# Joining 64-bit weights to fp32 with one join moved from VectorE to ScalarE

## The chip, the cores and the metric

One core of one Trainium2 chip runs the whole program. The metric is device time in microseconds of one execution. The kernel before took 991.16 us, the median of three runs (989.19 to 991.88).

## The reference

A linear-attention block and two MLPs on 2304 tokens of 512 features (batch 4, 8 heads, sequences of 576, head size 64, 128 random features):

```python
kv = np.einsum('bhsm,bhsd->bhmd', k_p, v)            # k_p, q_p = phi(k), phi(q): exp of a projection
out = np.einsum('bhsm,bhmd->bhsd', q_p, kv) / (np.einsum('bhsm,bhm->bhs', q_p, z)[..., None] + 1e-06)
x = ((x @ w_a) * (x @ w_b)) @ w_out                  # first MLP, d_ff 1536
h = np.maximum(x @ w_in, 0.0); y = (h * h) @ w_out2  # second MLP, d_ff 2048
```

The weights of both MLPs are the product of an fp32 array and an fp64 scalar, and so arrive as fp64. All products are wanted at fp32 quality.

## The kernel before

TensorE multiplies in fp32r, a rounded fp32. So each weight is cut in two parts, hi (its value cast to fp32r) and lo (the rest), and each product is made of three matmuls (hi·hi, hi·lo, lo·hi). Activations are cut in the same way.

**From fp64 to fp32.** A weight lies in memory as two 32-bit words. The kernel loads both (the tile raw, last index 0 for the low word, 1 for the upper) and puts the fp32 together from bits. ScalarE reads the upper word as if it were an fp32, scales it by a power of two (WORD_SCALE), and so shifts the exponent into place; the result is the tile a. VectorE then makes the tile p in three joins: a shifted left by 3 with the lowest bits masked off (`tensor_scalar`, line 187), the sign of a joined to it (line 191), and the three top bits of the low word (line 195, shifted right by 29). Then ScalarE casts p to hi (line 199) and VectorE subtracts to get lo (line 200).

**First MLP.** `split` does this, for 1024 elements a partition (the pair of w_a and w_b of one f) or 512 (one f of w_out). 12 f make 12 big and 12 small splits. `load_split` issues the loads on the sync engine SP into one of two raw buffers and puts the split on a list; the splits are spread over the first 175 us, beside the attention of the first batches and the first passes of the MLP. The tiles a and p have one buffer each. The order in which instructions stand on each engine is set by a list scheduler when the program is built. The work that stands beside the splits is: transposes of q and k that ScalarE copies out of PSUM (S, line 382), their projection (ps_p, line 329), minimum on VectorE (nm, line 333), exponential on ScalarE (qp and kp, line 335), transposes of qp copied out (qT, line 543), products with kv (ps_n, line 548) and quotients on VectorE; and of the MLP ab (line 696), the product a·b on ScalarE and VectorE (lines 800 to 803) and y (line 721). The kept hi and lo of w_a and w_b stay in the tile W; those of w_out go to a scratch in DRAM.

**Second MLP.** It uses a seven-product form of the matrix product. `unit` converts one j of w_in or w_out2 in two halves of 512 elements (lines 919 to 930, the same three joins into the area AB), makes four differences (line 939), and casts and subtracts each of seven blocks (lines 950 and 953). There are 16 units, so 32 halves. Eight units are made in the last pass of the first MLP (540 to 640 us) and eight in `in_step` (640 to 800 us), where ScalarE also copies the products pY and pW out of PSUM (line 1035) and VectorE adds (line 1038). From 800 us on the last product runs (line 1184), without units.

Of the kernel before, what the change touches and what calls it, by code (L numbers as in the profile page):

```python
# [11 lines left out]
U32 = mybir.dt.uint32  # L12
ACTF = mybir.ActivationFunctionType
ALU = mybir.AluOpType
# [10 lines left out]


WORD_SCALE = 2.0 ** -111
W_SCALE = 2.0 ** 8
Y_SCALE = 2.0 ** -24

# [5 lines left out]
def f32(ap):  # L36
    return ap.bitcast(F32)


def i32(ap):  # L40
    return ap.bitcast(I32)


@with_exitstack
def kernel(
# [13 lines left out]
    nc = tc.nc  # L59
# [119 lines left out]
    def split(raw, t):  # L179

        n = raw.shape[1]
        a = top["cut"].tile([128, 2, 512], F32, tag="a", name="a")[:, 0:n]
        p = top["cut"].tile([128, 2, 512], F32, tag="p", name="p")[:, 0:n]
        nc.scalar.activation(out=a, in_=f32(raw[:, :, :, 1]), func=ACTF.Copy, scale=WORD_SCALE)
        nc.vector.tensor_scalar(
            out=i32(p), in0=i32(a), scalar1=3, scalar2=0x7FFFFFF8,
            op0=ALU.logical_shift_left, op1=ALU.bitwise_and,
        )  # L190
        nc.vector.scalar_tensor_tensor(
            out=i32(p), in0=i32(a), scalar=-0x80000000, in1=i32(p),
            op0=ALU.bitwise_and, op1=ALU.bitwise_or,
        )
        nc.vector.scalar_tensor_tensor(
            out=p.bitcast(U32), in0=raw[:, :, :, 0].bitcast(U32), scalar=29,
            in1=p.bitcast(U32), op0=ALU.logical_shift_right, op1=ALU.bitwise_or,
        )
        nc.scalar.copy(out=t[:, :, 0, :], in_=p)  # L199
        nc.vector.tensor_tensor(  # L200
            out=t[:, :, 1, :], in0=p, in1=f32(t[:, :, 0, :]), op=ALU.subtract
        )
# [482 lines left out]
    def a_units():  # L685
# [80 lines left out]
        for n, (pi, f) in enumerate(todo):  # L766
# [27 lines left out]
            for o in range(0, g.shape[2], w_):  # L794
# [3 lines left out]
                else:  # L798
                    a_s = gpool.tile([128, w_], F32, tag="t", name="a_s", bufs=2)
                nc.scalar.mul(out=a_s, in_=aps[:, c], mul=1.0 / W_SCALE)  # L800
                nc.vector.tensor_tensor(out=a_s, in0=bps[:, c], in1=a_s, op=ALU.mult)  # L801
# [84 lines left out]
    def raw_at():  # L886
        return area["raw"][:, 0:2048].rearrange("p (h f w) -> p h f w", h=2, w=2)
# [17 lines left out]
    def unit(kind, j, dst, groups, nxt=None, stage=None):  # L905


        raw = raw_at()
        a = seg("AB", 0, 2, 512)
        bt = seg("AB", 4096, 8, 256)  # L910

        def load(h):
            unit_load(*nxt, h)

        ops = []
        for h in range(2):
            w = bt[:, 2 * h:2 * h + 2].rearrange("p a n -> p (a n)")
            ops += [
                lambda h=h: nc.scalar.activation(
                    out=f32(a[:, h]), in_=f32(raw[:, h, :, 1]), func=ACTF.Copy, scale=WORD_SCALE,  # L920
                ),
                lambda h=h, w=w: nc.vector.tensor_scalar(
                    out=i32(w), in0=i32(a[:, h]), scalar1=3, scalar2=0x7FFFFFF8,
                    op0=ALU.logical_shift_left, op1=ALU.bitwise_and,
                ),
                lambda h=h, w=w: nc.vector.scalar_tensor_tensor(
                    out=i32(w), in0=i32(a[:, h]), scalar=-0x80000000, in1=i32(w),
                    op0=ALU.bitwise_and, op1=ALU.bitwise_or,
                ),
                lambda h=h, w=w: nc.vector.scalar_tensor_tensor(  # L930
                    out=w.bitcast(U32), in0=raw[:, h, :, 0].bitcast(U32), scalar=29,
                    in1=w.bitcast(U32), op0=ALU.logical_shift_right, op1=ALU.bitwise_or,
                ),
            ]
            if nxt:
                ops.append(lambda h=h: load(h))

        def sub(o, x, y):
            nc.vector.tensor_tensor(
                out=f32(bt[:, o]), in0=f32(bt[:, x]), in1=f32(bt[:, y]), op=ALU.subtract  # L940
            )

        ops += [lambda t=t: sub(*t) for t in ((4, 0, 2), (6, 1, 0), (5, 1, 4), (7, 3, 5))]
        fill = []
        for g0, g1 in groups:
            o = {}

            def hi(g0=g0, g1=g1, o=o):
                o["t"] = dst(g0, g1)
                nc.scalar.copy(out=o["t"][:, :, 0], in_=f32(bt[:, 1 + g0:1 + g1]))  # L950

            def lo(g0=g0, g1=g1, o=o):
                nc.vector.tensor_tensor(
                    out=o["t"][:, :, 1], in0=f32(bt[:, 1 + g0:1 + g1]), in1=f32(o["t"][:, :, 0]),
                    op=ALU.subtract,
                )
                if kind == "out":
                    nc.sync.dma_start(out=wo2_d[:, g0:g1, j], in_=f32(o["t"]))

            fill += [hi, lo]  # L960
        return ops, fill
# [155 lines left out]
    OUTS = [("X", 0, B11), ("Y", 3, T4), ("X", 1, B21), ("W", 3, T1), ("Y", 0, T2), ("W", 1, B22), ("Y", 2, T3)]  # L1117
    ISC = 1.0 / W_SCALE

# [356 lines left out]
```

## Time and profile before

| | |
|---|---|
| median of three runs | 991.16 us |
| profiled execution, its own time | 989.96 us |
| its span, first to last instruction | 988.2 us |
| VectorE (DVE) busy | 662.4 us, 67% |
| ScalarE (ACT) busy | 534.1 us, 54% |
| granted TensorE clock | 1.0 throughout |

The span is what the trace covers; the 1.8 us around it belong to the execution too. An engine's busy time is the union of its instructions. Shares over the whole span are means over stages with different limits, so the windows by stage are of more use. A wait in the trace carries the instruction that ended it.

### The profile page before, as it was taken

The page shows a single profiled execution, that of the slowest core. Times are in us where ns is not written, and L with a number is a line of the kernel's source. Part 1 is how long each engine was busy: PE and PEld are TensorE (multiplying, and loading weights), DVE is VectorE, ACT ScalarE, POOL GpSimd, SP SyncE. Part 2 cuts the span into 40 slices and gives each one's busy share as a digit, 9 for nine tenths or more (in the row PEclk, how much of TensorE's full clock was granted, in tenths as well). Part 3 has the DMA queues.
Part 4 walks back from the last instruction along what each step waited for, and adds up shares of the span by engine and source line. Part 5 has one row for each costly group of instructions (what it writes and reads, how often), then busy time and mean ns, then how long its engine had stood idle before and what let it go on. Part 6 is the DMA issues. An engine that isn't in the chain of part 4 may idle for free.

```text
span 988.2 us, 17329 instructions
## 1 busy us (share of the span) xinstructions
PE 969.0 (98%) x6337; PEld 890.0 (90%) x6337; DVE 662.4 (67%) x1624; ACT 534.1 (54%) x1288; POOL 28.9 (3%) x54
## 2 busy tenths in 40 slices
PE   7899999999999999999999999999999999999998
PEld 6799998999998878788888888899999999999998
DVE  3888679765544444444443998988787347988794
ACT  5876556666554533243333554676676555455561
POOL 4000100000000000000000000000000000000000
PEclk9999999999999999999999999999999999999999
DMA  7766976634553111232123999337675599844301
GB/s 188 216 177 199 296 240 210 205 100 137 156 155 101 62 57 54 70 96 76 54 65 128 310 331 362 104 107 233 215 237 200 181 363 407 355 154 145 112 18 49
DMA packets 110358, 171.07 MB, mean 173 GB/s; under 512 B 27713, under 2 KB 83521, under 8 KB 107841
## 3 DMA queue, kind: packets, MB, share of 16 engines
q1 hardware_dynamic: 108736, 168.39, 51.1%
q0 software_dynamic: 1536, 1.58, 0.6%
q8 instruction: 50, 0.82, 0.3%
q14 instruction: 36, 0.29, 0.1%
HBM read 120.13 MB, written 49.81 MB: 172 GB/s over the span
## 4 chain that ended last, share of the span: by engine, by line
PE 78%; DVE 8%; DMA 7%; ACT 5%; issue 2%; SPq 0%; ACTq 0%; DVEq 0%
PE abw L696 14%; PE y L721 10%; PE pY L1026 9%; PE oY L1184 7%; PE ab L696 7%; PE oW L1184 5%; PE pW L1026 5%; PE oX L1184 4%; PE ps_n L548 3%; PE pX L1026 2%; PE ps_kv L482 2%; PE ps_p L329 2%; PE ps_p L404 2%; DMA raw<-in_moe_w_b_dram 2%; PE ps_qt L539 2%
## 5 line engine op out<-in xcount | busy, mean ns | idle before, releaser
L696 PE MATMUL abw<-x_all,W 128*128 128x512 f32 x576 | 142.6, 395 | 0.0
L721 PE MATMUL y<-gs,wo 128*128 128x256 f32 (+1 forms) x720 | 138.1, 332 | 0.2 <-ACT wo L199 0.2
L696 PEld LDWEIGHTS abw<-x_all,W 128*128 128x128 f32 x576 | 105.7, 188 | 20.5
L721 PEld LDWEIGHTS y<-gs,wo 128*128 128x128 f32 x720 | 108.8, 189 | 11.2 <-ACT wo L199 0.6
L696 PE MATMUL ab<-x_all,W 128*128 128x256 f32 x576 | 87.5, 292 | 1.4 <-DVE W L200 0.9
L696 PEld LDWEIGHTS ab<-x_all,W 128*128 128x128 f32 x576 | 74.8, 189 | 3.0 <-DVE W L200 1.5
L696 PE MATMUL abw<-x_mid,W 128*128 128x512 f32 x288 | 71.2, 395 | 0.0
L696 PEld LDWEIGHTS abw<-x_mid,W 128*128 128x128 f32 x288 | 52.5, 188 | 10.4
L415 DVE CUSTOM_DVE_ANT_0 c<-ps_p,c 128x128 f32<-128x128 f32 x152 | 38.3, 286 | 25.0 <-ACT c L413 24.2
L802 ACT CAST gs<-a_s 128x256 fp32r<-128x256 f32 x84 | 33.0, 407 | 30.4 <-DVE a_s L801 29.2
L413 ACT COPY c<-ps_p 128x256 f32<-128x256 f32 x76 | 27.8, 372 | 36.6 <-PE ps_p L404 36.2
L1026 PE MATMUL pY<-W,M 128*128 128x384 f32 x240 | 45.9, 335 | 0.0
L801 DVE TENSOR_TENSOR a_s<-abw,a_s 128x256 f32<-128x256 f32 x48 | 18.1, 419 | 38.2 <-PE abw L696 38.2
L1184 PE MATMUL oW<-W 128*128 128x256 f32 x360 | 43.0, 276 | 0.0
L1026 PEld LDWEIGHTS pY<-W,M 128*128 128x128 f32 x240 | 41.9, 188 | 0.4 <-ACT F L1035 0.3
L1184 PEld LDWEIGHTS oW<-W 128*128 128x128 f32 x360 | 41.8, 188 | 0.2 <-DVE W L1152 0.2
L1151 ACT CAST W<-F 128x384 fp32r<-128x384 f32 x57 | 29.0, 513 | 23.5 <-PE oX L1184 10.6
L696 PE MATMUL ab<-x,W 128*128 128x256 f32 x288 | 41.3, 287 | 0.0
L800 ACT ACTIVATE a_s<-abw 128x256 f32<-128x256 f32 x48 | 17.4, 387 | 42.6 <-PE abw L696 42.5
L1043 ACT ACTIVATE F<-F 128x384 f32<-128x384 f32 x48 | 24.5, 518 | 24.8 <-DVE F L1038 24.7
L548 PEld LDWEIGHTS ps_n<-kvr,qT 128*128 128x128 f32 x256 | 32.3, 191 | 5.9 <-ACT qT L543 3.3
L420 ACT ACTIVATE qp<-c,nm 128x128 f32<-128x128 f32 x88 | 31.0, 397 | 11.4 <-DVE nm L415 10.3
(212 smaller groups left out, 2146.0 us busy)
## 6 DMA issues: line engine op xcount, KB each, us to landing
wo<-wo_d SPq DMA_DIRECT2D x60, 512.0 KB, 3.6
s_d<-F SPq DMA_DIRECT2D x24, 768.0 KB, 5.6
raw<-in_moe_w_out_dram SPq DMA_DIRECT2D x32, 256.0 KB, 4.7
raw<-in_moe_w_in_dram SPq DMA_DIRECT2D x16, 512.0 KB, 6.4
W<-wo_d SPq DMA_DIRECT2D x4, 2048.0 KB, 14.9
F<-s_d SPq DMA_DIRECT2D x5, 1536.0 KB, 7.8
raw<-in_moe_w_a_dram SPq DMA_DIRECT2D x12, 512.0 KB, 3.8
raw<-in_moe_w_b_dram SPq DMA_DIRECT2D x12, 512.0 KB, 5.2
```

What stands on the lines that cost most here:

```text
L329: state["proj"] = nc.tensor.matmul(ps[:, 2 * x:2 * x + 2].rearrange("p h m -> p (h m)"), lhsT=s, rhs=OMZ.rearrange("p h m -> p (h m)"), st ...
L413: nc.scalar.copy(out=c, in_=ps[:, :, 1, :])
L415: nc.vector.tensor_tensor_reduce(out=c[:, x, :], in0=ps[:, x, 0, :], in1=c[:, x, :], scale=1.0, scalar=3.0e38, op0=ALU.add, op1=ALU.min, a ...
L420: nc.scalar.activation(out=dst[:, 2 * n + x, :], in_=c[:, x, :], func=ACTF.Exp, scale=-1.0, bias=nm[:, x:x + 1],)
L548: lambda x=x: nc.tensor.matmul(pn[:, x, :], lhsT=t["qT"][:, x % 2 * len(g) + x // 2, :], rhs=kv[:, x % 2, :], start=True, stop=True,)
L696: nc.tensor.matmul(ps, lhsT=wv[:, s_, kc, :], rhs=x[..., kc, m_, :], start=(kc == 0 and (s_, m_) == TERMS[0]), stop=(kc == KC - 1 and (s_, ...
L721: nc.tensor.matmul(y_part(pi, f, c), lhsT=wo[pi, f][:, s_, c * 128:(c + 1) * 128], rhs=g[:, m_, :],  start=(f == f0 and (wide or c % 2 == ...
L802: nc.scalar.copy(out=g[:, 0, c], in_=a_s)
L1026: nc.tensor.matmul(p, lhsT=w[:, s_, 128 * kk:128 * kk + 128], rhs=y[:, ai, kk, m_, :], start=(c not in seen and kk == 0 and (s_, m_) == TE ...
L1043: nc.scalar.activation(out=t[:, o], in_=t[:, o], func=ACTF.Relu)
L1151: ahead_of["cast"] = nc.scalar.copy(out=sop[:, 0], in_=src)
L1184: nc.tensor.matmul(tiles_of(p, t), lhsT=sops[n][:, s_, 128 * t:128 * t + 128], rhs=w[:, m_, :], start=(fresh and k == 0 and (t % 2 == 0 or ...
```

## The change

VectorE's first join (`tensor_scalar`) is gone. ScalarE now has two operations where it had one. The new one reads the top 16 bits of the low word, scales by 2^-13 with a bias and writes the result as int32 into p: the three bits as an integer. The other still scales the upper word into a, with the absolute value, so that the sign is gone and nothing has to be masked. VectorE's two joins are then a shifted by 3, joined with p, and the sign bit taken from the raw upper word, joined with p. The same in `split` and in `unit`.

```diff
+LOW_SCALE = 2.0 ** -13
+LOW_BIAS = 2.0 ** -14 - 0.5
...
+def top16(raw):
+
+    return raw.bitcast(mybir.dt.uint16)[..., 1]
...
-        nc.scalar.activation(out=a, in_=f32(raw[:, :, :, 1]), func=ACTF.Copy, scale=WORD_SCALE)
-        nc.vector.tensor_scalar(
-            out=i32(p), in0=i32(a), scalar1=3, scalar2=0x7FFFFFF8,
-            op0=ALU.logical_shift_left, op1=ALU.bitwise_and,
+        nc.scalar.activation(
+            out=i32(p), in_=top16(raw), func=ACTF.Copy, scale=LOW_SCALE, bias=LOW_BIAS
+        )
+        nc.scalar.activation(out=a, in_=f32(raw[:, :, :, 1]), func=ACTF.Abs, scale=WORD_SCALE)
+        nc.vector.scalar_tensor_tensor(
+            out=i32(p), in0=i32(a), scalar=3, in1=i32(p),
+            op0=ALU.logical_shift_left, op1=ALU.bitwise_or,
         )
         nc.vector.scalar_tensor_tensor(
-            out=i32(p), in0=i32(a), scalar=-0x80000000, in1=i32(p),
+            out=i32(p), in0=raw[:, :, :, 1], scalar=-0x80000000, in1=i32(p),
             op0=ALU.bitwise_and, op1=ALU.bitwise_or,
-        )
-        nc.vector.scalar_tensor_tensor(
-            out=p.bitcast(U32), in0=raw[:, :, :, 0].bitcast(U32), scalar=29,
-            in1=p.bitcast(U32), op0=ALU.logical_shift_right, op1=ALU.bitwise_or,
         )
```

In `unit` the same five operations of each half are edited in the same way, with `w`, a part of the area AB, in the place of p.

The scheduler puts the instructions of all engines in a new order. Three places of ScalarE's queue follow. In them p and a are the split's two tiles, W and wo what it makes, S, T and qT copies of transposes, x_all and x copies of the attention's output, a_s and gs the MLP's product, kp and qp exponentials. The first is the start, at about 19 us: before, and then the change.

```order
L335 ACTIVATE kp<-ps_p,nm 128x128 x4
L186 ACTIVATE a<-raw 128x1024
L382 COPY S<-ps_t_313 128x256
L569 CAST x_all<-ps_x 128x256
L382 COPY S<-ps_t_328 128x512
L319 COPY T<-ps_tt 128x128
L186 ACTIVATE a<-raw 128x512
```

```order
L343 ACTIVATE kp<-ps_p,nm 128x128 x4
L195 ACTIVATE p<-raw 128x1024
L198 ACTIVATE a<-raw 128x1024
L577 CAST x_all<-ps_x 128x256
L390 COPY S<-ps_t_313 128x256
L390 COPY S<-ps_t_328 128x512
L327 COPY T<-ps_tt 128x128
L198 ACTIVATE a<-raw 128x512
```

The split's two operations stand together, and the short copy S has moved behind x_all. The second place is ScalarE's queue at about 112 us, before and with the change.

```order
L462 COPY kvt<-ps_kt 128x130
L800 ACTIVATE a_s<-ab 128x256
L186 ACTIVATE a<-raw 128x1024
L802 CAST gs<-a_s 128x256
L382 COPY S<-ps_t_1472 128x512
L335 ACTIVATE kp<-ps_p,nm 128x128 x4
```

```order
L470 COPY kvt<-ps_kt 128x130
L808 ACTIVATE a_s<-ab 128x256
L390 COPY S<-ps_t_1472 128x512
L195 ACTIVATE p<-raw 128x1024
L198 ACTIVATE a<-raw 128x1024
L810 CAST gs<-a_s 128x256
L343 ACTIVATE kp<-ps_p,nm 128x128 x4
```

The copy S has moved from behind the split to ahead of it; gs now stands behind two operations. The third place is ScalarE's queue at about 144 us.

```order
L335 ACTIVATE qp<-ps_p,nm 128x128 x2
L186 ACTIVATE a<-raw 128x1024
L543 COPY qT<-ps_qt 128x256
L382 COPY S<-ps_t_1931 128x128
L800 ACTIVATE a_s<-ab 128x256
```

```order
L343 ACTIVATE qp<-ps_p,nm 128x128 x2
L551 COPY qT<-ps_qt 128x256
L390 COPY S<-ps_t_1931 128x128
L195 ACTIVATE p<-raw 128x1024
L198 ACTIVATE a<-raw 128x1024
L808 ACTIVATE a_s<-ab 128x256
```

The copies qT and S have moved ahead of the split.

## Rows read from the trace of the kernel before

**Rows 1.** The page's first part: busy us, share of the span, instructions

```profile
PE 969.0 (98%) x6337; PEld 890.0 (90%) x6337; DVE 662.4 (67%) x1624; ACT 534.1 (54%) x1288; POOL 28.9 (3%) x54
```

**Rows 2.** Windows by stage: length, busy time and instructions by engine, clock, DMA

```profile
18.00:48.00 30.00, 26.23 (x174) 22.12 (x175) 23.00 (x45) 23.22 (x65) 3.55 (x6) 1.00 0.61 181
48.00:84.00 36.00, 35.83 (x282) 34.04 (x281) 31.72 (x65) 26.32 (x68) 3.49 (x6) 1.00 0.64 195
84.00:122.00 38.00, 36.82 (x293) 35.63 (x292) 25.55 (x47) 23.03 (x57) 3.59 (x6) 1.00 0.83 262
...
140.00:180.00 40.00, 37.43 (x294) 35.05 (x293) 34.81 (x89) 25.17 (x62) 2.34 (x4) 1.00 0.74 237
...
540.00:640.00 100.00, 99.84 (x448) 83.22 (x447) 91.34 (x159) 55.80 (x87) 0.00 (x0) 1.00 0.80 279
640.00:800.00 160.00, 160.00 (x924) 159.72 (x923) 115.07 (x210) 107.10 (x230) 0.00 (x0) 1.00 0.59 201
```

**Rows 3.** Waits of TensorE, 18 to 180 us: total us, times, longest

```profile
PE ps_p L329 <- ACT S L382: 2.2, 2, 1.2
PE ps_n L548 <- ACT qT L543: 1.6, 2, 0.9
...
PE ab L696 <- DVE W L200: 0.9, 2, 0.8
...
PE ab L696 <- ACT W L199: 0.4, 1, 0.4
```

**Rows 4.** Groups by line and form: busy us, mean ns, idle before

```profile
L186 ACT ACTIVATE a<-raw 128x1024 f32<-128x1024 f32 x12 | 13.9, 1156 | 6.7 <-DMA raw<-in_moe_w_b_dram 4.7 <-DVE p L191 2.0
L186 ACT ACTIVATE a<-raw 128x512 f32<-128x512 f32 x12 | 8.2, 680 | 5.5 <-DVE den L523 1.7 <-DVE p L191 1.4 <-issue 1.0
L919 ACT ACTIVATE AB<-raw 128x512 f32<-128x512 f32 x32 | 21.1, 669 | 15.7 <-DMA raw<-in_moe_w_in_dram 10.1 <-DMA raw<-in_moe_w_out_dram 4.9 <-PE y L721 0.5
L187 DVE TENSOR_SCALAR p<-a 128x1024 int32<-128x1024 int32 x12 | 8.3, 689 | 5.2 <-ACT a L186 5.2
L922 DVE TENSOR_SCALAR AB<-AB 128x512 int32<-128x512 int32 x32 | 12.8, 421 | 4.1 <-ACT AB L919 4.0
L191 DVE SCALAR_TENSOR_TENSOR p<-a,p 128x1024 int32<-128x1024 int32 x12 | 14.6, 1217 | 0.1
```

**Rows 5.** Timeline at the start: start us, us, engine, line, idle before

```profile
19.77 1.25 ACT L186 ACTIVATE a<-raw 128x1024 f32<-128x1024 f32 x1
20.81 0.46 ACT L382 COPY S<-ps_t 128x256 f32<-128x256 f32 x1
22.81 0.37 ACT L569 CAST x_all<-ps_x 128x256 fp32r<-128x256 f32 x1 [1.54 <-PE ps_x L561]
23.08 0.59 ACT L382 COPY S<-ps_t 128x512 f32<-128x512 f32 x1
23.73 1.59 PEld L329 LDWEIGHTS ps_p<-OMZ,S 128*128 128x128 f32 x8 [0.48 <-ACT S L382]
```

**Rows 6.** Timeline at 113 us

```profile
112.83 1.14 ACT L186 ACTIVATE a<-raw 128x1024 f32<-128x1024 f32 x1 [0.71 <-DMA raw<-in_moe_w_b_dram]
114.16 0.58 ACT L382 COPY S<-ps_t 128x512 f32<-128x512 f32 x1
114.79 0.48 PE L329 MATMUL ps_p<-OMZ,S 128*128 128x256 f32 x1 [0.94 <-ACT S L382]
```

**Rows 7.** Timeline from 144 to 152 us

```profile
144.49 1.13 ACT L186 ACTIVATE a<-raw 128x1024 f32<-128x1024 f32 x1 [1.34 <-DMA raw<-in_moe_w_b_dram]
145.94 0.32 PE L548 MATMUL ps_n<-kvr,qT 128*128 128x65 f32 x1 [0.72 <-ACT qT L543]
...
151.58 0.39 PE L696 MATMUL ab<-x_all,W 128*128 128x256 f32 x1 [0.76 <-DVE W L200]
```

**Rows 8.** Timeline at 724 us, in the second MLP's first product

```profile
724.57 0.86 ACT L1035 COPY F<-pY 128x384 f32<-128x384 f32 x2 [0.15 <-PE pY L1026]
...
726.45 0.85 PE L1026 MATMUL pY<-W,M 128*128 128x384 f32 x4
```

More of the change, by code (lines that the diff above doesn't have):

```diff
@@ L918, in unit @@
             ops += [
+                lambda h=h, w=w: nc.scalar.activation(
+                    out=i32(w), in_=top16(raw)[:, h], func=ACTF.Copy, scale=LOW_SCALE, bias=LOW_BIAS,
+                ),
                 lambda h=h: nc.scalar.activation(
[L920 to L924, printed above, removed]
+                    out=f32(a[:, h]), in_=f32(raw[:, h, :, 1]), func=ACTF.Abs, scale=WORD_SCALE,
                 ),
                 lambda h=h, w=w: nc.vector.scalar_tensor_tensor(
-                    out=i32(w), in0=i32(a[:, h]), scalar=-0x80000000, in1=i32(w),
-                    op0=ALU.bitwise_and, op1=ALU.bitwise_or,
+                    out=i32(w), in0=i32(a[:, h]), scalar=3, in1=i32(w),
+                    op0=ALU.logical_shift_left, op1=ALU.bitwise_or,
                 ),
                 lambda h=h, w=w: nc.vector.scalar_tensor_tensor(
-                    out=w.bitcast(U32), in0=raw[:, h, :, 0].bitcast(U32), scalar=29,
-                    in1=w.bitcast(U32), op0=ALU.logical_shift_right, op1=ALU.bitwise_or,
+                    out=i32(w), in0=raw[:, h, :, 1], scalar=-0x80000000, in1=i32(w),
+                    op0=ALU.bitwise_and, op1=ALU.bitwise_or,
                 ),
```

## The prediction

> **What bounds the kernel now.** I read the busy shares first. TensorE is busy for 969.0 of 988.2 us [rows 1], so all that any change off TensorE can win is about 19 us, and only where TensorE stands still. The windows by stage say where that is and where the joins are [rows 2]. In the first MLP's weight stage (18 to 180 us, 24 splits) TensorE is idle 3.77 us of 30 (18 to 48), 0.17 of 36, 1.18 of 38 and 2.57 of 40: 7.69 us together (122 to 140, not shown, adds nothing). In the two stretches with the second MLP's units it is idle 0.16 us of 100 and 0.00 us of 160. So VectorE, busy 91.34 of 100 us from 540 on, is nearly full there and yet holds nobody up: time taken off it in that stretch buys nothing.
>
> Then the waits of TensorE from 18 to 180 us [rows 3]: it waited 2.2 us for ScalarE's copy S, 1.6 us more for the copy qT, and only 0.9 + 0.4 us for a finished weight (W, from VectorE and from ScalarE). What ends TensorE's waits is ScalarE more than VectorE, and ScalarE is the engine that gets more work.
>
> **The change part by part.** *Removed:* one join on VectorE for each split or half unit: 12 of 0.689 us, and 12 + 32 of half that size at 0.421 us, 8.3 + 5.1 + 13.5 = 26.9 us by the means and a little less where they overlap [rows 4]. It is the cheapest of the three: the join that stays (two inputs) takes 1.217 us for the same 1024 elements [rows 4]. *Added:* one ScalarE operation for each. The trace of before has no 16-bit read and no integer write on ScalarE. The nearest rows are its own scaled copies of the upper word, which read with the same stride of 8 bytes: 1.156, 0.680 and 0.669 us [rows 4]. I take these for the new operation, and for the absolute value too, which replaces a copy of the same size: busy 13.9 + 8.2 + 21.1 = 43.2 us of ScalarE. A bound from above is twice that, if a 16-bit read or the conversion cost double; from below, half.
>
> The Trainium skill (ScalarE: Activation LUTs, section What ACT_TABLE_LOAD costs) gives 186 ns and 0.833 ns an element for an ACTIVATE with immediate scale and bias, which makes an estimated 1.039 us for 1024 elements. The row's 1.156 us is longer [rows 4]; by the page each place below would cost about a tenth less, which moves the sum by less than 0.2 us.
>
> The chain of one split, raw to hi cast, is ScalarE, three joins, ScalarE. Before: 1.156 + 0.689 + 2 × 1.217 = 4.28 us to the last join's end (the third join has the second's two inputs and size); now 2 × 1.156 + 2 × 1.217 = 4.75 us, 0.47 us longer where nothing else waits. Where VectorE was behind with other work, the chain is shorter instead, by up to 0.69 us. I take zero for the waits on W: the longest, 0.76 us at 151.58 us [rows 7], could grow by 0.47 or shrink by 0.69 us.
>
> The first new wait: p and a are single buffers, and p is now first written by ScalarE. It must wait for VectorE's last subtraction of the split before, where until now VectorE followed itself. What is queued behind that on ScalarE are copies of PSUM and exponentials that TensorE waits for. The program's order was made again with the new operations in it, so it moved some of these copies ahead and some behind. Three places carry the sum:
>
> - *Start (18 to 48 us).* The first big split's operation ran at 19.77 us and the two copies S at 20.81 and 23.08 us; TensorE's weight load stood 0.48 us for the second [rows 5]. In the new order both operations stand ahead, and the short copy S has moved behind x_all, which starts at 22.81 us: so the long S comes some 0.46 us later (the length of the short one). +0.5 us. Four more operations are added in this stretch, 1.156 + 3 × 0.680 = 3.2 us. ScalarE is idle 6.78 us of 30 here [rows 2], and VectorE gets 2 × 0.689 + 3 × 0.421 = 2.6 us back. I take a third of the 3.2 as on the path, +1.0 us. Bounds: -2.6 us (all that VectorE gets back), +4.35 us (all five, 2 × 1.156 + 3 × 0.680).
> - *At 113 us.* The split's operation waited 0.71 us for its weights and ran 1.14 us, the copy S stood behind it, and TensorE idled 0.94 us for that copy [rows 6]. In the new order S stands ahead of the split. -0.9 us. Bounds: 0 and -1.18, the idle time of that stretch.
> - *At 145 us.* The same with the copy qT: behind the split's operation, TensorE idle 0.72 us [rows 7]; now ahead. -0.7 us. Bounds: 0 and -2.57, all idle time of that stretch.
>
> From 180 to 540 us there is no split: nothing. From 540 to 640 us VectorE gets relief, TensorE has 0.16 us to win: nothing. From 640 to 800 us ScalarE goes from 107.10 to about 117.8 of 160 us (16 × 0.669), and each eviction may find one more operation ahead of it. The copy of pY ran 724.57 to 725.43 us and TensorE came back to pY at 726.45 us [rows 8]: 1.02 us of slack against 0.669 us. Zero, and if this cover goes, the third rival below.
>
> Sum: 0.5 + 1.0 - 0.9 - 0.7 = -0.1 us. It is made against the profiled execution, 989.96 us with a span of 988.2 us; that one lies 1.2 us under the median of 991.16 us. **Forecast: 991.1 us** beside that median, that is, no change. About 0.3% (3 us, so 988.2 to 994.1 us) is what a measurement of this kernel can tell from none.
>
> **Rivals.** *ScalarE takes VectorE's place (slower).* The start is the place where TensorE waits for ScalarE, and ScalarE is already busy 23.22 of 30 us there, as VectorE is with 23.00 [rows 2]; the change adds 4.35 us to the one and takes 2.6 us from the other. If all five operations lie in the path, the start costs 4.35 us and not 1.5; and if the copies at 113 and 145 us find another split ahead, their 1.6 us are not won: 991.1 + 2.85 + 1.6 = 995.5 us. It decides once two more of the four count in full. For it: rows 3, and the price, 1.156 us added for each 0.689 us removed. Against it: ScalarE's 6.78 us of idle time, and the copies that moved ahead. The Trainium skill says the same as a rule (ScalarE: Activation LUTs, section Rules for kernel authors): simple elementwise work belongs on VectorE, not on ScalarE. Chance 0.14.
>
> *VectorE was the brake (faster).* From 48 to 84 us and from 140 to 180 us VectorE is busy 31.72 of 36 and 34.81 of 40 us [rows 2]; a join less for each split lets its other work, the minima and quotients on which the exponentials wait, come earlier. If half of TensorE's 7.69 us idle time comes back: 991.16 - 3.8 = 987.3 us. Against it: the waits that VectorE ended are 0.9 us of those in rows 3. Chance 0.10.
>
> *The evictions come late (slower).* From 640 to 800 us, should two new operations, 1.34 us, stand ahead of a copy of pY, or one that waits for VectorE, 0.32 us are lost over the slack of 1.02 us. With eight units of two halves, 16 × 0.32 = 5.1 us, 996.2 us. Against it: one operation fits into the slack. Chance 0.05.
>
> **How the numbers follow.** No change has 0.71. The bounds of the three places add up to -6.35 and +4.35 us; half of each, as all three will not go one way, makes its own range 988.2 (where its 0.3% end) to 993.3 us. Faster by over 0.3% is the second rival, 0.10; slower is the first and the third, 0.19. The range goes from 988.2 us, under which lies the second rival, to 995.6 us, which takes the first in; left out are 0.10 and 0.05.
>
> **What would show it.** VectorE about 26 us less busy, ScalarE about 43 us more; the new operation near 1.16, 0.68 and 0.67 us; the waits for S at 113 us and qT at 145 us gone; more waits for ScalarE's copies before 48 us; TensorE's idle time unchanged past 540 us. Wrong, if the new operation takes over 2 us for 1024 elements, if TensorE's idle time before 180 us goes under 4 us or over 11 us, or if it stands still from 640 to 800 us.

## The result, and the profile after

| | before | changed |
|---|---|---|
| median, runs taken together | 989.79 us (6 runs, 988.51 to 991.88) | 995.07 us (6 runs, 993.63 to 996.57) |
| ratio, 95% interval | | 1.0054 (1.0039 to 1.0068) |
| profiled execution, its span | 989.96 us, 988.2 us | 996.57 us, 994.8 us |

The change makes the kernel slower by 0.54%, 5.3 us, outside the forecast's 0.3%; 995.07 us lies in the stated range only because that was drawn wide enough to take in the first rival. The profiled execution of the change lies 1.5 us above its median, so its trace shows a little more loss than the typical run has.

The prices were right. The page's first part after, beside [rows 1], and the groups by line and form (busy us, mean ns, idle before), beside [rows 4]:

```profile
PE 974.2 (98%) x6337; PEld 893.8 (90%) x6337; DVE 641.6 (64%) x1568; ACT 568.6 (57%) x1344; POOL 28.7 (3%) x54
```

```profile
L195 ACT ACTIVATE p<-raw 128x1024 int32<-128x1024 uint16 x12 | 13.8, 1151 | 0.5 <-DVE W L208 0.5
L195 ACT ACTIVATE p<-raw 128x512 int32<-128x512 uint16 x12 | 8.2, 687 | 2.1 <-DVE W L208 2.1
L927 ACT ACTIVATE AB<-raw 128x512 int32<-128x512 uint16 x32 | 21.4, 672 | 7.9 <-DMA raw<-in_moe_w_out_dram 3.8 <-DMA raw<-in_moe_w_in_dram 3.5 <-PE y L729 0.5
L198 ACT ACTIVATE a<-raw 128x512 f32<-128x512 f32 x12 | 8.4, 698 | 4.5 <-DVE p L199 4.5
```

The new operation takes 1.151, 0.687 and 0.672 us (forecast 1.16, 0.68, 0.67): a 16-bit read and an integer result cost no more than the fp32 copy. The windows by stage, beside [rows 2] (length, busy us and instructions of PE, PEld, DVE, ACT and POOL, granted clock, DMA share, GB/s):

```profile
18.00:48.00 30.00, 26.07 (x168) 22.63 (x167) 20.04 (x38) 26.25 (x69) 3.51 (x6) 0.94 0.56 166
48.00:84.00 36.00, 34.44 (x265) 32.55 (x264) 27.45 (x56) 29.13 (x70) 3.49 (x6) 1.00 0.61 181
84.00:122.00 38.00, 37.50 (x296) 35.94 (x295) 25.35 (x45) 26.14 (x61) 3.50 (x6) 1.00 0.81 259
122.00:140.00 18.00, 17.86 (x148) 17.37 (x148) 12.98 (x21) 13.35 (x28) 0.00 (x0) 1.00 0.67 203
140.00:180.00 40.00, 37.84 (x279) 34.92 (x279) 31.89 (x76) 28.72 (x67) 2.32 (x4) 0.96 0.70 232
...
640.00:800.00 160.00, 158.85 (x909) 157.05 (x909) 110.14 (x195) 113.79 (x243) 0.00 (x0) 1.00 0.56 188
```

TensorE's idle time from 18 to 180 us went from 7.69 us to 3.93 + 1.56 + 0.50 + 0.14 + 2.16 = 8.29 us, only 0.6 us more. The new thing is the column of the clock: 0.94 and 0.96 where before had 1.00. At the lower level (1.2 GHz, 0.50) half of the time is lost, so these windows lose 0.06 × 30 + 0.04 × 40 = 3.4 us. Together 4.0 us. And that is how far the trace stands behind: the last x_mid of the attention and, at the end of the second MLP's first product, the first cast of the last product, in before and after:

```profile
420.79 0.29 DVE L623 TENSOR_TENSOR x_mid<-ps_xt,x_mid 128x128 fp32r<-128x128 f32 x1 [0.82 <-ACT x_mid L622]
...
784.37 0.52 ACT L1151 CAST W<-AB 128x384 fp32r<-128x384 f32 x1 [0.70 <-PE pW L1026]
```

```profile
424.81 0.29 DVE L631 TENSOR_TENSOR x_mid<-ps_xt,x_mid 128x128 fp32r<-128x128 f32 x1 [0.81 <-ACT x_mid L630]
...
790.97 0.52 ACT L1158 CAST W<-AB 128x384 fp32r<-128x384 f32 x1 [0.70 <-PE pW L1033]
```

The lag is 4.02 us at 421 us and 6.60 us at 784 us, and the spans differ by 6.6 us. So in this execution 4.0 us are lost in the first MLP's splits and 2.6 us more in the second MLP.

**Where the clock fell.** Windows of 4 us after:

```profile
36.00:40.00 4.00, 2.95 (x25) 2.76 (x25) 2.33 (x5) 4.00 (x12) 0.00 (x0) 0.99 0.71 247
40.00:44.00 4.00, 3.85 (x16) 3.17 (x15) 2.92 (x6) 1.86 (x4) 0.00 (x0) 0.59 0.44 120
```

```profile
152.00:156.00 4.00, 2.56 (x14) 1.51 (x12) 3.67 (x8) 3.18 (x8) 0.00 (x0) 0.99 0.48 137
156.00:160.00 4.00, 3.73 (x20) 3.74 (x21) 2.65 (x6) 2.52 (x5) 2.32 (x4) 0.58 0.69 229
```

TensorE had stood still 1.05 and 1.44 us of 4 just before the clock fell. Each fall lasted (0.01 + 0.41) × 4 / 0.5 = 3.4 us, so it took half of that, 1.7 us. What it waited for there, and in the third place, at 62 us, the timeline of after tells (start, duration, idle before and what ended it):

```profile
36.67 1.17 ACT L195 ACTIVATE p<-raw 128x1024 int32<-128x1024 uint16 x1
...
37.67 0.64 ACT L551 COPY qT<-ps_qt 128x512 f32<-128x512 f32 x1
...
38.37 1.11 PE L556 MATMUL ps_n<-kvr,qT 128*128 128x65 f32 x8 [1.05 <-ACT qT L551]
```

```profile
58.77 1.22 DVE L203 SCALAR_TENSOR_TENSOR p<-raw,p 128x1024 int32<-128x1024 int32 x1
...
61.10 1.12 ACT L198 ACTIVATE a<-raw 128x1024 f32<-128x1024 f32 x1 [0.99 <-DMA raw<-in_moe_w_b_dram]
62.13 1.03 ACT L207 CAST W<-p 128x1024 fp32r<-128x1024 f32 x1
...
63.21 0.50 PE L704 MATMUL ab<-x_all,W 128*128 128x256 f32 x2 [1.11 <-ACT W L207]
```

```profile
150.95 1.22 DVE L199 SCALAR_TENSOR_TENSOR p<-a,p 128x1024 int32<-128x1024 int32 x1
...
152.20 0.68 ACT L198 ACTIVATE a<-raw 128x512 f32<-128x512 f32 x1 [0.51 <-DVE p L199]
...
153.33 0.28 ACT L327 COPY T<-ps_tt 128x128 f32<-128x128 f32 x1
...
153.67 0.70 PE L337 MATMUL ps_p<-OMZ,T 128*128 128x256 f32 x2 [1.39 <-ACT T L327]
```

Three times a split's operation stands in ScalarE's queue ahead of something TensorE needs. At 37 us it is the new operation itself, ahead of qT. At 62 us the cast of W, whose p was made at 59.99 us, stands behind the next split's upper-word operation, which waits 0.99 us for words that have not landed. At 152 us an upper-word operation waits 0.51 us for VectorE's first join, because a has one buffer, and the copy T is behind it (with two more short operations between). The waits of TensorE from 18 to 180 us (total, times, longest), beside [rows 3]:

```profile
PE ps_p L337 <- ACT T L327: 1.4, 1, 1.4
PE ps_p L337 <- ACT S L390: 1.3, 2, 0.7
PE ab L704 <- ACT W L207: 1.1, 1, 1.1
PE ps_n L556 <- ACT qT L551: 1.1, 1, 1.1
...
PE ab L704 <- DVE W L208: 0.7, 2, 0.5
```

From 640 to 800 us TensorE's matmuls now stand still 1.15 us and its weight loads wait 2.7 us (0.3 us before), always for a copy of pY. This is one:

```profile
717.17 1.32 PE L1033 MATMUL pY<-W 128*128 128x384 f32 x6 [0.30 <-ACT F L1042]
```

### The profile page after: what moved, and what is told of

Read it like the earlier page. It is cut to its first block, busy times and chain, and to the rows that moved or that the text cites. A ratio compares the mean times of both kernels' runs of the same rounds, so it can differ in the third digit from the quotient of the medians.

```text
span 994.8 us, 17321 instructions
## 1 busy us (share of the span) xinstructions
PE 974.2 (98%) x6337; PEld 893.8 (90%) x6337; DVE 641.6 (64%) x1568; ACT 568.6 (57%) x1344; POOL 28.7 (3%) x54
## 4 chain that ended last, share of the span: by engine, by line
PE 79%; DMA 7%; ACT 6%; DVE 6%; issue 2%; SPq 0%; DVEq 0%; ACTq 0%
PE abw L704 18%; PE y L729 13%; PE ab L704 8%; PE oY L1191 7%; PE pY L1033 5%; PE oW L1191 5%; PE oX L1191 4%; DMA raw<-in_moe_w_in_dram 3%; PE ps_n L556 3%; PE ps_kv L490 3%; PE pW L1033 2%; PE ps_p L412 2%; PE ps_p L337 2%; PE ps_qt L547 2%; DMA F<-s_d 1%
## 5 line engine op out<-in xcount | busy, mean ns | idle before, releaser
L808 ACT ACTIVATE a_s<-abw 128x256 f32<-128x256 f32 x48 | 17.4, 387 | 43.4 <-PE abw L704 43.3
L704 PEld LDWEIGHTS ab<-x,W 128*128 128x128 f32 x288 | 36.7, 189 | 0.1
```

The source lines that it names most:

```text
L704: nc.tensor.matmul(ps, lhsT=wv[:, s_, kc, :], rhs=x[..., kc, m_, :], start=(kc == 0 and (s_, m_) == TERMS[0]), stop=(kc == KC - 1 and (s_, ...
```

## The experiments

My theory when I began was that ScalarE's added 43 us are the cost, in two separate places, the splits and the second MLP's units (A). The rivals: it is only the clock (C), VectorE's relief matters more (V), and the place of the new operation, with what it waits for and what stands behind it, is the cost, and not its time (O). All were compared with the kernel before on the same chip; "clock" is the mean over a kernel's runs of the granted clock, which for before was 0.998 to 0.999.

| kernel | ratio to before (95%) | clock |
|---|---|---|
| the change | 1.0054 (1.0039 to 1.0068) | 0.997 |
| first MLP alone | 1.0054 (1.0033 to 1.0075) | 0.995 |
| second MLP alone | 1.0005 (0.9994 to 1.0016) | 1.000 |
| no low word | 1.0000 (0.9982 to 1.0017) | 0.996 |
| low word on GpSimd, both MLPs | 1.0044 (1.0025 to 1.0063) | 0.998 |
| low word on GpSimd, first MLP | 1.0003 (0.9988 to 1.0018) | 0.999 |
| change + spare matmuls | 1.0033 (1.0014 to 1.0051) | 0.999 |
| before + spare matmuls | 1.0034 (1.0016 to 1.0051) | 0.999 |
| three joins + low word | 1.0226 (1.0198 to 1.0254) | 0.988 |
| the same, into raw | 1.0212 (1.0189 to 1.0234) | 0.992 |
| low word into raw, both MLPs | 1.0120 (1.0101 to 1.0138) | 0.996 |
| low word into raw, first MLP | 1.0102 (1.0086 to 1.0119) | 0.997 |
| GpSimd into raw, first MLP | 1.0052 (1.0033 to 1.0070) | 0.998 |
| low word behind upper, into p, first MLP | 1.0061 (1.0037 to 1.0084) | 0.995 |
| low word behind upper, into raw, first MLP | 1.0001 (0.9987 to 1.0015) | 0.998 |
| new form from the sixth split on | 1.0030 (1.0015 to 1.0045) | 0.999 |
| new form in the first five splits | 1.0020 (1.0003 to 1.0036) | 0.997 |
| behind upper, into raw; units as changed | 0.9998 (0.9982 to 1.0015) | 0.999 |
| behind upper, into raw; three joins, first MLP | 1.0067 (1.0040 to 1.0093) | 0.998 |

**Which MLP.** The first kernel takes only the change in `split`, the second only the one in `unit`; the other function stays as in the kernel before. In the first, against the change:

```diff
-                lambda h=h, w=w: nc.scalar.activation(
-                    out=i32(w), in_=top16(raw)[:, h], func=ACTF.Copy, scale=LOW_SCALE, bias=LOW_BIAS,
-                ),
                 lambda h=h: nc.scalar.activation(
-                    out=f32(a[:, h]), in_=f32(raw[:, h, :, 1]), func=ACTF.Abs, scale=WORD_SCALE,
+                    out=f32(a[:, h]), in_=f32(raw[:, h, :, 1]), func=ACTF.Copy, scale=WORD_SCALE,
                 ),
...
```

> New join in the splits of the first MLP alone, the second MLP's units as before. Theory A (ScalarE is handed 43 us and holds the TensorE back in two separate places): the trace of the change lies 4.03 us behind the trace of before all the way from 190 to 530 us, so this kernel is +4.0 us (993.8), with a granted clock of 0.5 near 40 and 156 us again and no idle TensorE in 640-800 us. Theory B (the loss is all in the second MLP's evictions, the early lag is noise of one profiled run): within 0.7 us of before, clock 1.00. Theory C (it is only the two stretches at half clock, 3.4 us each, which cost 1.7 us each): +3.4 us.

> New join in the second MLP's units alone, the first MLP's splits as before. Theory A: +2.6 us (992.4), TensorE waits for the copies out of PSUM (line of F<-pY) in 640-800 us, about 1.1 us of idle there; clock 1.00 before 180 us. Theory C (the half clock alone): no change, 989.8 plus or minus 0.7. If both parts add, this and the kernel with the first MLP alone sum to the change's +5.3 to +6.6 us.

The whole loss is in the first MLP, and the second MLP's part is within what can be told from nothing. The first kernel's own runs show how much goes with the clock: 993.03 us at a mean clock of 0.999, 999.65 us at 0.989. The second corrects the reading of the trace: in it TensorE stood still 0.14 us from 640 to 800 us and not 1.15, with the same operations on ScalarE (114.76 us busy against 113.79):

```profile
640.00:800.00 160.00, 159.86 (x917) 158.59 (x916) 109.19 (x193) 114.76 (x245) 0.00 (x0) 1.00 0.60 200
```

The 2.6 us of the one profiled execution of the change were not a cost of every run; what made the difference there stays open.

**Load or relief.** Two kernels go beside each other: one drops the low word's operation, and with it the three lowest bits (the first join becomes a shift alone); one keeps before's three joins and adds the low word's operation to them, so that ScalarE's load grows and no join is saved. That operation writes p as in the change, so the wait for p comes with it.

```diff
-        nc.scalar.activation(
-            out=i32(p), in_=top16(raw), func=ACTF.Copy, scale=LOW_SCALE, bias=LOW_BIAS
-        )
...
-        nc.vector.scalar_tensor_tensor(
-            out=i32(p), in0=i32(a), scalar=3, in1=i32(p),
-            op0=ALU.logical_shift_left, op1=ALU.bitwise_or,
-        )
+        nc.vector.tensor_scalar(
+            out=i32(p), in0=i32(a), scalar1=3, scalar2=None, op0=ALU.logical_shift_left,
+        )
```

> The change in both MLPs without the low word: ScalarE's added operation is gone, VectorE's first join is a shift alone, so the three lowest bits of each word are left out of what is computed. ScalarE has as many operations as before, VectorE one join fewer than before. Theory A (the added ScalarE time costs it): 989.8 plus or minus 1.0, clock 1.00 throughout, no waits for copies in 640-800 us; ScalarE near 534 us busy, VectorE near 640. Rival V (VectorE was the brake): 987 or below. Rival O (it is the new order of the dependences, not the load: the upper-word operation writes the one buffer that the first join reads): 993 to 995, with the same waits as the change.

The other, against the kernel before (the same in `unit`):

```diff
+        nc.scalar.activation(
+            out=i32(p), in_=top16(raw), func=ACTF.Copy, scale=LOW_SCALE, bias=LOW_BIAS
+        )
         nc.scalar.activation(out=a, in_=f32(raw[:, :, :, 1]), func=ACTF.Copy, scale=WORD_SCALE)
```

> Before with its three VectorE joins, plus the low-word operation of ScalarE in both MLPs, whose result the first join overwrites: the added ScalarE load without the saved join. With the kernel that has neither (one ScalarE operation, two joins) this fills a table of two by two. Theory A (the ScalarE operation costs, the join is worth little): 995 to 998, the time of the change or up to 3 us more. Rival O (the new dependences of the change cost it, not the load): within 1 us of before.

Without the added operation the loss is gone, though not the falls of the clock, and the time is that of before. Its mean clock, 0.996, is as low as the change's 0.997, so a low clock by itself does not make a kernel slower than before. Where the clock held, the relief may be worth something: of its 12 runs the two shortest, 986.04 and 986.65 us, both had a clock of 0.999, and the longest, 994.14 us, had 0.993. The added operation without the saved join costs 22 us, four times what the change costs. So the saved join is worth far more beside the new operation than without it: the two do not add up, and none of the theories says that. Since the order of the queue differs in each of these kernels, they do not part an operation's time from its place.

**The clock.** 26 spare matmuls were put where TensorE stood still in the trace of the change, for example:

```diff
             pn = at_bank([128, 2 * len(g), D + 1], "ps_n")
+            if b == 0 and chunks == (0, 1) and p:
+                fill(pn.rearrange("p a d -> p (a d)")[:, 0:256], 3, 256)
```

> The change plus 26 spare matmuls on TensorE that no result uses (4 ahead of the first ps_kv, 3 ahead of ps_n of pairs 1 to 3 of the start, 8 ahead of the third ab, 5 ahead of the tail projection of q at about 152 us), where TensorE stood still in the trace of the change. They add work and take no wait away. Theory C (what the change costs is above all the granted clock of 0.5 for two stretches of 3.4 us, 1.7 us each, which follow idle TensorE): clock 1.00 or one stretch at most, 992 or below, faster than the change although it computes more. Theory W (the waits for ScalarE are the cost, the clock no more than a sign of them): 995 to 999, the change's time plus up to 4 us for the spare matmuls that cover no wait.

> The kernel before with the same 26 spare matmuls. Its clock was 1.00 without them, so they can only cost: both theories expect 990 to 993.5, clock 1.00, no gain. If it is faster than before by over 1 us, the runs of before lose time to the clock as well (5 of its 24 runs had a mean of 0.998 or less, with spans of 990.2 to 992.2 against a median near 988.4).

With spare matmuls the change kept its clock, 1.00 in every window below, where the first and the last had 0.94 and 0.96:

```profile
18.00:48.00 30.00, 29.56 (x194) 25.89 (x194) 21.49 (x42) 26.67 (x71) 3.49 (x6) 1.00 0.60 180
...
140.00:180.00 40.00, 38.34 (x294) 35.84 (x293) 31.96 (x78) 28.41 (x66) 2.34 (x4) 1.00 0.75 242
```

It came out between the two theories. The ratio to before fell from 1.0054 to 1.0033, although the same spare matmuls cost the kernel before 0.34%. With spare matmuls in both, the change is no slower than before: 1.0033 and 1.0034. That speaks for the clock as a part of the loss. It is not a clean proof, since the spare matmuls changed the order too and the intervals of the change with and without them overlap.

How large a part can be estimated from the single runs. Beside all the experiments, on several chips, 23 runs of before had a mean clock of 0.996 or 0.997, as all six of the change have; they took 992.7 us on average, and the 80 with 0.999 or 1.000 took 989.6 us. The change's 995.07 us is 2.4 us above the first and 5.5 us above the second, so a little over half of the loss goes with the clock and the rest does not.

**On GpSimd.** The same arithmetic for the low word, on the engine that has most room.

```diff
-        nc.scalar.activation(
-            out=i32(p), in_=top16(raw), func=ACTF.Copy, scale=LOW_SCALE, bias=LOW_BIAS
-        )
+        nc.gpsimd.tensor_scalar(
+            out=i32(p), in0=top16(raw), scalar1=LOW_SCALE, scalar2=LOW_BIAS,
+            op0=ALU.mult, op1=ALU.add,
+        )
```

> The change with the low word's operation on GpSimd instead of ScalarE, in both MLPs (same arithmetic, result as in the change). Theory A: ScalarE's load is as before and VectorE still has a join fewer, so 988 to 991 if the GpSimd operation takes up to about 3 us for 1024 elements; no half clock. Rival V (VectorE was the brake): 987. Rival G (the chain to the joins grows by the GpSimd operation, or GpSimd slows VectorE): 993 or more, with VectorE waits for GpSimd's p and longer VectorE operations than 1.23 us.

> The low word's operation on GpSimd in the first MLP's splits, and the second MLP's units as before. The kernel with GpSimd in both MLPs lay only 0.14 us behind before from 230 to 540 us and lost 4.3 us in 640 to 760 us, so with the units as before: 988.5 to 991. Theory A: same as before within 0.3%, with a clock of 1.00 in most runs. Rival G (GpSimd's operation is too slow for the splits): 993 or more. A gain of over 1.5 us would say that the saved join is worth something where ScalarE doesn't pay for it.

In the splits it costs nothing, as A expected. It writes p there too, and up to 180 us GpSimd waited far longer for VectorE's last read of p than ScalarE's 2.6 us in the change (most of it for the big splits):

```profile
POOL p L195 <- DVE W L209: 57.5, 11, 7.0
```

That wait was free. The likely reason is that little stood behind it: GpSimd has 54 instructions of its own in the whole kernel [rows 1]. In both MLPs the operation on GpSimd costs 0.44%, as rival G has it, so here the units do cost: TensorE waited 2.6 us for copies of pY. The GpSimd operation takes 1.150 us for 1024 elements, and in the units VectorE's first join became slower beside it, 758 ns against 686:

```profile
L935 DVE SCALAR_TENSOR_TENSOR AB<-AB 128x512 int32<-128x512 int32 x32 | 24.1, 758 | 10.6 <-POOL AB L928 9.5 <-ACT AB L932 1.0
```

**Where the result is written.** To take p out of the wait, the low word's result was written over the low word itself.

```diff
-            out=i32(p), in_=top16(raw), func=ACTF.Copy, scale=LOW_SCALE, bias=LOW_BIAS
+            out=raw[:, :, :, 0], in_=top16(raw), func=ACTF.Copy, scale=LOW_SCALE, bias=LOW_BIAS
...
-            out=i32(p), in0=i32(a), scalar=3, in1=i32(p),
+            out=i32(p), in0=i32(a), scalar=3, in1=raw[:, :, :, 0],
```

> The change with ScalarE's low-word result written over the low word it was made from, in the raw tile, not into the single tile p (and not into the second MLP's joined buffer); the first join reads it there. ScalarE and VectorE do the same work as in the change, but ScalarE need no longer wait until VectorE has read p for the split before. Rival O (the cost is that dependence: a ScalarE operation that stands in its queue for VectorE's last read of p, with the copies for TensorE behind it): 988 to 991, clock 0.999 or 1.00 in most runs. Theory A (the cost is ScalarE's added time): 994 to 996, as the change. A strided write that is dearer than 1.16 us for 1024 elements would add to either.

> The same in the first MLP's splits alone, the second MLP's units as before. Rival O: 987 to 990 (a gain if the saved join is worth what the kernel without a low word showed where its clock held: spans of 984.3 and 984.9 us at a clock of 0.999). Theory A: 993.5 to 995, as the change in the first MLP alone.

> The low word by GpSimd in the first MLP's splits, written into the raw tile, units as before. With p as its place it was the same as before (1.0003). Rival O: GpSimd can start as soon as the words have landed, so the chain to the joins loses its wait for p; 986.5 to 989.5. Theory A: as with p, 989 to 991.

The last has all three joins; its third takes the low word's bits from raw, shifted by 0.

> Before's three VectorE joins plus ScalarE's low-word operation written into the raw tile (the third join takes it from there, shifted by 0). With p as its place the same added operation cost 21 us. Rival O (dependence on p): the 21 us shrink to 1 to 6 us, since the operation needs nothing but the landed words. Theory A (ScalarE's time itself, 43 us of it): 1008 or more.

Rival O missed all four. The first three are slower than with p, which A did not expect either; the last is as slow, as A has it. The timeline of the first shows one reason:

```profile
15.36 0.65 ACT L195 ACTIVATE raw<-raw 128x512 int32<-128x512 uint16 x1 [6.93 <-DMA raw<-in_moe_w_out_dram]
15.91 2.16 ACT L343 ACTIVATE kp<-ps_p,nm 128x128 f32<-128x128 f32 x8
...
16.32 0.69 PE L490 MATMUL ps_kv<-V,kp 128*128 128x65 f32 x2 [5.62 <-ACT kp L343]
```

With no p to wait for, the operation stands ahead of eight exponentials. On the chip its words had not landed; ScalarE stood 6.93 us, with the exponentials behind it, and TensorE 5.62 us. The wait for p, it seems, had kept the operation back. That place is about half of this kernel's loss of some 12 us, and in the kernel with GpSimd no such wait stands there; its loss was not followed up. So this did not test the wait for p; it showed how much one place in the queue can cost.

**The place.** Next the low word's operation was issued behind the upper word's, once into p and once into raw, in the first MLP alone.

```diff
-        nc.scalar.activation(
-            out=i32(p), in_=top16(raw), func=ACTF.Copy, scale=LOW_SCALE, bias=LOW_BIAS
-        )
-        nc.scalar.activation(out=a, in_=f32(raw[:, :, :, 1]), func=ACTF.Abs, scale=WORD_SCALE)
+        ab = nc.scalar.activation(out=a, in_=f32(raw[:, :, :, 1]), func=ACTF.Abs, scale=WORD_SCALE)
+        with tc.issue_after(ab.ins):
+            nc.scalar.activation(
+                out=raw[:, :, :, 0], in_=top16(raw), func=ACTF.Copy, scale=LOW_SCALE, bias=LOW_BIAS
+            )
...
-            out=i32(p), in0=i32(a), scalar=3, in1=i32(p),
+            out=i32(p), in0=i32(a), scalar=3, in1=raw[:, :, :, 0],
```

> The change in the first MLP alone, with the low-word operation issued behind the upper-word operation on ScalarE instead of ahead of it. Load theory (A): 993 to 996, as with the change in the first MLP alone (995.9). Place theory (O: the operation that waits for VectorE's last read of p stands ahead of the copies for TensorE): 990 to 992 if the order helps; behind the upper word it must wait for p as well, so at most 2 us of gain.

> The same order, and the low-word result written into the raw tile. It needs nothing but the landed words then, and stands behind the upper-word operation that needs them too, so neither p nor a late load holds the queue. Theory A (ScalarE's 28 us in the first MLP are the cost): 993 to 996. Theory O (the wait for p): 988 to 991. The 5.6 us wait of the first kernel with the raw tile, between the start and 20 us, is to be gone in either case.

With the same operations on ScalarE (551.0 and 551.6 us busy) the kernel that writes p is 0.61% slower than before and the one that writes raw 0.01%. Four kernels of the first MLP alone now differ by place and buffer:

| low-word operation | into p | into raw |
|---|---|---|
| ahead of the upper word | 1.0054 | 1.0102 |
| behind the upper word | 1.0061 | 1.0001 |

So ScalarE's added load does not by itself make the loss, and neither the place alone nor the buffer alone mends it; both together do. (O expected 990 to 992 us for the place alone, which took 996.61, and 988 to 991 us for both, which took 989.08.) ScalarE's waits from 18 to 180 us in its split operations, for the change and for the kernel that writes raw:

```profile
ACT a L198 <- DVE p L199: 5.3, 6, 1.6
ACT W L207 <- DVE p L203: 5.3, 7, 1.4
ACT wo L207 <- DVE p L203: 2.9, 3, 1.5
ACT p L195 <- DVE W L208: 2.6, 3, 1.3
```

```profile
ACT a L195 <- DVE p L200: 4.1, 4, 2.8
ACT a L195 <- DMA raw<-in_moe_w_out_dram: 3.1, 3, 1.7
ACT a L195 <- DMA raw<-in_moe_w_b_dram: 2.7, 3, 1.8
ACT W L208 <- DVE p L204: 1.3, 2, 1.1
ACT wo L208 <- DVE p L204: 0.8, 1, 0.8
```

The kernel that writes p behind the upper word has the change's waits: 2.6 us for p, 5.1 and 2.9 us in the casts. In the one that writes raw the wait for VectorE's last read of p is gone, and the casts wait less (1.3 + 0.8 us against 5.3 + 2.9): other work now stands ahead of them. Windows of the kernel that writes raw:

```profile
18.00:48.00 30.00, 27.59 (x178) 23.05 (x177) 22.48 (x42) 27.40 (x72) 3.49 (x6) 1.00 0.62 195
48.00:84.00 36.00, 34.80 (x275) 33.00 (x275) 29.20 (x58) 31.50 (x74) 3.49 (x6) 1.00 0.57 187
...
140.00:180.00 40.00, 38.88 (x307) 36.44 (x307) 32.38 (x88) 28.83 (x69) 2.32 (x4) 1.00 0.73 248
```

ScalarE is busier than in the change from 18 to 84 us (58.90 against 55.38 us) and TensorE idle less (3.61 against 5.49 us), at full clock. How much of the gain is the wait itself and how much the new order, these runs can't part.

Nor is all of it ScalarE's queue. The kernel that writes p behind the upper word has a mean clock of 0.995, and in its profiled execution it was 0.77 from 18 to 48 us, which loses 0.23 × 30 = 6.9 us. There TensorE had waited at 17 to 19 us for the load of V; by the trace the DMA ended that wait and no split's operation (with raw it was 0.3 us):

```profile
PE ps_kv L491 <- DMA V<-in_v_dram: 1.9, 1, 1.9
...
18.00:48.00 30.00, 26.55 (x146) 23.30 (x146) 17.78 (x32) 22.43 (x59) 3.49 (x6) 0.77 0.53 153
```

The kernel with the first MLP alone has the same in its trace (1.8 us, then 0.77). Why V came later there no run shows. At like clock (0.997) the kernel that writes p took 995.96 us in one run and the one that writes raw 989.89 and 991.92 us in two, so a difference of about 5 us is left without the clock.

**Which splits.** In `split`, the new form by a count:

```diff
+        top["n"] = top.get("n", 0) + 1
+        if top["n"] > 5:
...
```

> First MLP: the first five splits (to about 55 us) joined as before, the other nineteen by the new form; units as before. By the trace of the change the lag grows by 1.7 us at 40 us, by 2.3 at 55 to 65 and by 1 at 150 to 160, with a stretch at half clock at 40 and at 156. If the cost is paid in the start: 990 to 991.5. If it is paid later (the splits at 60 and 150 us): 992.5 to 994. If the whole is ScalarE's time, spread over the splits: 4 to 5 us times 19 of 24 splits, 993 to 994.

And the other way round, `top["n"] <= 5`:

> First MLP: the first five splits by the new form, the others as before. If the cost is paid in the start: 992 to 994, with a stretch at half clock near 40 us. If later: 989.5 to 991. The two parts are to add up to the 5 us of the change in the first MLP; a sum that falls short says that the parts depend on each other through the order of the queue.

Neither half is free: 0.30% and 0.20%, together 0.50% of the 0.54%. The loss is spread, and the intervals do not say that one half is the dearer. The kernel with the new form from the sixth split on loses its 0.30% at the mean clock of before, 0.999, and in its profiled execution (993.51 us) the clock was 1.00 from 18 to 980 us: waits of this kind cost without the clock too.

**The mended change, and its load alone.** The first is the change with the `split` that writes raw behind the upper word. The second is the kernel before with that one operation more in `split`:

```diff
-        nc.scalar.activation(out=a, in_=f32(raw[:, :, :, 1]), func=ACTF.Copy, scale=WORD_SCALE)
+        ab = nc.scalar.activation(out=a, in_=f32(raw[:, :, :, 1]), func=ACTF.Copy, scale=WORD_SCALE)
+        with tc.issue_after(ab.ins):
+            nc.scalar.activation(
+                out=raw[:, :, :, 0], in_=top16(raw), func=ACTF.Copy, scale=LOW_SCALE, bias=LOW_BIAS
+            )
...
-            out=p.bitcast(U32), in0=raw[:, :, :, 0].bitcast(U32), scalar=29,
+            out=p.bitcast(U32), in0=raw[:, :, :, 0].bitcast(U32), scalar=0,
```

> The whole change, with the splits' low word written into the raw tile behind the upper-word operation; the second MLP's units as in the change. Place theory: 989 to 991.5, against 995 for the change itself, since the second MLP's part alone measured 1.0005. If the units cost 2.6 us, as the one trace of the change has it between 640 and 760 us: 992.

> First MLP: before's three VectorE joins, and ScalarE's low-word operation added in the raw tile behind the upper-word operation (28 us of ScalarE, no join saved); units as before. If ScalarE's time is free in itself: 989 to 991. If the saved join pays for it: 994 or more; with the operation on p, or ahead of the upper word, it was 1012 and 1009 in both MLPs.

The whole change with the mended split is as fast as before, with ScalarE at 568.2 and VectorE at 641.3 us, the loads of the change. Its page's first part:

```profile
PE 970.5 (98%) x6337; PEld 890.5 (90%) x6337; DVE 641.3 (65%) x1568; ACT 568.2 (58%) x1344; POOL 28.8 (3%) x54
```

Keep the third join beside the operation and it costs 0.67%. So, as far as two kernels with different orders can be compared, ScalarE's time is not free in itself; in the first MLP the saved join pays for it, and nothing is left over. No version tried is measurably faster than before.

## Why the prediction was wrong

- *Prices and busy times: right.* VectorE 20.8 us less, ScalarE 34.5 us more by the page; less than 26 and 43, because busy time counts overlap once and the new operation's own times add up to the forecast's (13.8 + 8.2 + 21.4 = 43.4 us).
- *The places at 113 and 145 us: right in kind.* From 84 to 122 us TensorE's idle time fell by 0.68 us (1.18 to 0.50; forecast 0.9). From 140 to 180 us it fell by 0.41 us (forecast 0.7): the copy qT no longer stood behind a split, but the copy T at 153 us now did, 1.39 us.
- *The start, +1.5 us: wrong in kind.* Idle time from 18 to 48 us grew by 0.16 us, not 1.5. The stretch lost 1.8 us to the clock instead. (The shown lines of [rows 3] leave out one more wait for qT, of 1.1 us; with it ScalarE's copies S and qT ended 4.9 us of TensorE's waits before, not 3.8.)
- *The "first new wait" was named and got no price: the step that failed.* The prediction says that ScalarE must now wait for VectorE to be done with p, with copies for TensorE behind it, and then prices three places by the lengths of operations and of before's own waits. With the same ScalarE work the split that writes p behind the upper word cost 0.61%, and 0.01% with raw in the place of p; in the trace of the change ScalarE waited 2.6 us for p and 8.2 us in the casts of W and wo (4.8 us before).
- *"I take zero for the waits on W": the same step, seen from TensorE.* From 48 to 84 us idle time rose from 0.17 to 1.56 us, for the cast of W at 63 us (1.11 us) and the subtraction behind it. The chain's length, 4.75 against 4.28 us, was the wrong measure. The cast waited not for the joins but for its turn, behind an operation that waited for a DMA.
- *The sum had no term for the clock: a term that was missing.* All terms together, as idle time, came to +0.6 us, near the -0.1 us of the forecast, but by luck: 1.5 us at the start that did not come stand against 1.4 us from 48 to 84 us that did. In this pair of traces another 3.4 us came from the granted clock, which the profile of before shows at 1.00 in every window of [rows 2], and which I took as given; over all runs the estimate above gives the clock a little over half of the loss. All six runs of the change have a mean of 0.996 or 0.997.
- *First rival (ScalarE takes VectorE's place, 995.5 us): near in the time, by luck.* 995.07 us was measured, but neither of its terms came: the start cost 0.16 us of idle time and 1.8 us of clock, not 4.35 us, and at 113 and 145 us the copies did not find another split ahead. The same ScalarE operations, placed otherwise, cost nothing. By the rule of the Trainium skill (ScalarE: Activation LUTs, section Rules for kernel authors) simple elementwise work belongs on VectorE. The prices agree with it (0.689 us for the join that went, 1.151 us for the operation that came), and so does the time of the change (1.0054); the time of the mended change does not (0.9998).
- *Second rival (VectorE was the brake): not seen.* A join less and nothing added measured 1.0000; its two shortest runs, 4.2 and 3.6 us under before's median of 990.21 us, leave a small worth open that the clock took back.
- *Third rival (evictions late): seen in one trace*, 1.15 us of idle time, but the second MLP's part measured 1.0005. GpSimd in the units brings it out.
- *Of the marks of a wrong forecast*, only the last was met (TensorE standing still from 640 to 800 us). Idle time before 180 us, 8.29 us, stayed within 4 to 11 us and would have passed: idle time alone was the wrong mark.

## What to carry to other kernels

When an operation moves to another engine, ask less for its time than for what it waits for there and what stands behind it in that queue: the same ScalarE work cost 0.0% or 1.0% here, by the buffer that it wrote and its place, and the same wait cost nothing on GpSimd, whose queue has little behind it. A single buffer written by a second engine is a wait across engines; dropping it can let a scheduler issue the operation before its data have landed, so give it a free place and an anchor both. And where waits of about a microsecond crowd, look at the granted clock of the next stretch, which in the trace of the change took 1.7 us more after each of two such waits.

## What was not expected of the hardware

- The clock fell after short waits. In the change it fell to 1.2 GHz for 3.4 us after TensorE had been idle 1.05 us of 4. Yet in the trace of before it stayed at 2.4 GHz after 1.21 us of 4:

```profile
32.00:36.00 4.00, 2.79 (x20) 2.30 (x19) 2.94 (x6) 3.79 (x10) 1.17 (x2) 1.00 0.51 97
```

  So idle time in such a stretch does not decide it alone, and no run here shows what does. The kernel before has it too: in 5 of its 24 runs beside the first experiments the mean clock was 0.998 or less, and in 13 of 28 beside the second. So a clock of 1.00 in one profile does not promise it for the next run.
- ScalarE reads 16-bit words at a stride of 8 bytes and writes integers as fast as it copies fp32: 1151 against 1156 ns for 1024 elements.
- GpSimd did the same operation in the splits in the same time, 1150 ns, and left VectorE's joins there as they were, 1221 ns; in the units it took 925 ns for 512 elements, where ScalarE took 672.
